# An attention and MoE kernel: where the second matmul's sums of batch 0 lie in PSUM, and one line in the dealing of its pieces

## The chip, the cores and the metric

The kernel runs on one core of a Trainium2 chip. The metric is the device time of one execution in microseconds, as a median over several executions; lower is better. A profile of one execution gives the time of every instruction on each engine: TensorE (PE; its weight loads are shown apart as PEld), VectorE (DVE), ScalarE (ACT), GpSimd (POOL), and the queue of SyncE (SP), which issues most of the transfers.

## The reference, cut to what matters

Attention with a hash mask comes first (4 batches, 8 heads, 768 rows, 64 columns a head). Its output is the input of a two-matmul layer with SiLU between.

```python
def _attn_ref(q, k, v, proj):
    # q, k, v: (4, 8, 768, 64); proj: (64, 6)
    # ... a 6-bit bucket for each row of q and k, by the signs of q@proj and k@proj
    mask = q_bucket[:, :, :, None] == k_bucket[:, :, None, :]
    scores = np.where(mask, scale * np.matmul(q, k.transpose(0, 1, 3, 2)), -1000000000.0)
    # ... softmax
    return np.matmul(attn, v)

def _moe_ref(x, w_in, w_out):          # x: (3072, 512), w_in: (512, 2048), w_out: (2048, 512)
    h = x @ w_in
    g = h * (1.0 / (1.0 + np.exp(-h)))
    return g @ w_out
```

## The kernel before

The kernel is one long software pipeline. The attention is cut into 288 units, nine a head, so 72 units a batch (`BST = 72`). In the loop below, `w` counts them. A unit multiplies one block of exponentials with `v` (`av(w)`) and then makes the scores of the unit three ahead (`score(w + LEAD)`), whose exponential ScalarE takes at once. The layer's work of a batch is cut into pieces and dealt into the units of the next batch: batch 0's pieces go into units 65 to 160 and a few later ones.

PSUM has eight banks, and the kernel splits them by tag: three banks "s" (scores), three banks "m" (first matmuls, projections, transposes) and two banks "o" (attention sums). A bank of a tag is given to the next tile when the tile before it has been read for the last time.

```python
    def score(w):
        # ... pts: one block of 512 columns, or two of 256
        sp = ps.tile([P, 512], F32, tag="s", name="s_ps", bufs=LEAD)      # LEAD = 3
        for jt, c0, n, o0 in pts:
            nc.tensor.matmul(sp[:, o0 : o0 + n], t[:, S + jt * P : S + (jt + 1) * P],
                             t[:, c0 : c0 + n], start=True, stop=True)     # L381
        u = upl.tile([P, 512], F16, tag="u", name="u")
        nc.scalar.activation(out=u, in_=sp, func=AF.Exp, scale=ESC)        # L384
        ut[w] = u
    # ...
    def av(w):
        # ... four matmuls of 65 columns into o_ps, with u of this unit as weights   # L413
```

A piece of the first matmul (`mm1`) holds an "m" bank through four matmuls of 512 columns (or eight of 256), a tanh on ScalarE and a multiplication on VectorE that is issued a unit later:

```python
        def mm1(ci, grp, dts=slice(0, NDT)):
            # ...
                hp = ps.tile([P, 2, f, n // 2], F32, tag="m", name="h_ps", bufs=3)
            # ... matmuls over dt                                                    # L478
            nc.scalar.activation(out=th, in_=hp, func=AF.Tanh, scale=0.5)            # L488
            # ... later: g = (th + 1) * hp on VectorE                                # L491
```

The projection of two later pairs of heads takes two "m" banks at once, one after the other:

```python
    def proj_unit(*pairs):
        # ...
        for c0, w in ((0, 512), (512, S - 512)):
            bp = ps.tile([P, 512], F32, tag="m", name="bp_ps", bufs=3)
            # ... matmuls                                                            # L295
        # ... then one VectorE instruction for each of the two banks                 # L301
```

Batch 0's second matmul treats its larger chunk, 512 of the 768 rows, in four tiles of 128 rows, each a sum over 16 slices of `w_out`, in four pieces of four matmuls. The sum stays in one bank from the first piece to the last, and VectorE then takes it out:

```python
        def whole(t, part):

            if part == 0:
                banks[t] = ps.tile([P, DMODEL], F32, tag="s", name="o2_ps", bufs=3)
            op = banks[t]
            for ft in range(4 * part, 4 * part + 4):
                x = blk[0, ft // NK][:, t // 2, ft % NK, t % 2 * P : (t % 2 + 1) * P]
                nc.tensor.matmul(op, x, w_out16[:, ft, :],                           # L560
                                 start=(ft == 0), stop=(ft == NFT - 1))
            if part == 3:
                o = ops.tile([P, DMODEL], F32, tag="osb", name="osb", bufs=3)
                nc.vector.tensor_scalar(out=o, in0=op, scalar1=half_g, scalar2=None,
                                        op0=ALU.mult)                                # L564
                # ... and a transfer to the output
```

The dealing, with what it does for units 77 to 143 (for batch 0, `moe_list(0)` gives 32 pieces at unit 77):

```python
    for w in range(NW):
        flush()
        for fn in at.pop(w, []):                 # planned work: loads, projections, casts
            fn()
        if w % BST == 1:
            moeq.extend(moe_head())              # six left-over pieces of the batch before
        if w == BST + 5 or w % BST == 11 and w > 2 * BST:
            credit = 0.5
            moeq.extend(moe_list(w // BST - 1))
        keep = 3 if w >= NW - 12 else 0
        left = BST - w % BST
        n = -(-(len(moeq) - keep) // left) if len(moeq) > keep else 0
        in_head = w > 2 * BST and w % BST < 11
        credit += max(len(moeq) - keep, 0) / left
        skip = credit < 0.999 or w % QST in ((20, 21) if w > 2 * BST else (24, 25))
        if w > 2 * BST and w % BST < 11:
            skip = w % BST in (0, 2, 5, 7, 10)
        if n == 1 and len(moeq) - keep < left and skip:
            n = 0
        credit -= n
        for _ in range(n):
            moeq.popleft()()
        av(w)
        if w + LEAD < NW:
            score(w + LEAD)
```

Two more lines matter for what follows. `x_unit(p)` turns the attention's output of head pair `p` into `xT`, the input of the first matmul, by a transposing transfer of the SP queue (L448), for pair 7 planned at unit 146. `mm1` of batch 1 begins at unit 155 and reads `xT` of pairs 4 to 7.

Of the kernel before, what the change touches and what calls it, by code (L numbers as in the profile page):

```python
# [9 lines left out]
F32 = mybir.dt.float32  # L10
# [7 lines left out]
def kernel(  # L18
# [13 lines left out]
    NT, DMODEL = out.shape  # L32
    DFF = moe_w_in.shape[1]
    P = 128
# [23 lines left out]
    ps = ctx.enter_context(tc.tile_pool(name="ps", bufs=1, space=bass.MemoryType.PSUM))  # L58
# [316 lines left out]
    def score(w):  # L375
        h, pts = parts(w)
        p, par = divmod(h, 2)
        t = QKA[p % NSL] if par == 0 else QKB[p % NSL]
        sp = ps.tile([P, 512], F32, tag="s", name="s_ps", bufs=LEAD)
# [6 lines that stand above are left out]
# [68 lines left out]
    def flush():  # L454
        for fn in after:
            fn()
        after.clear()

    def moe_units(b):
# [55 lines left out]
        banks, kept = {}, {}  # L515
# [37 lines left out]
        def whole(t, part):  # L553

            if part == 0:
                banks[t] = ps.tile([P, DMODEL], F32, tag="s", name="o2_ps", bufs=3)
            op = banks[t]
            for ft in range(4 * part, 4 * part + 4):
                x = blk[0, ft // NK][:, t // 2, ft % NK, t % 2 * P : (t % 2 + 1) * P]
# [6 lines that stand above are left out]
                dst = out[b * S : (b + 1) * S, :].rearrange("(p t) n -> p t n", p=P)  # L566
                nc.sync.dma_start(out=dst[:, t, :], in_=o)
# [13 lines left out]
        if b == 0:  # L581
            big = [lambda t=t, part=part: whole(t, part) for t in range(4) for part in range(4)]
        else:
            big = [lambda n=n, t=t: product(0, n, t)
                   for n in (1, 2, 6, 5, 3, 7, 4) for t in range(2)]
            first[13] = then(first[13], (0, 1, lo))
            for grp, c in ((0, (0, 1, hi)), (1, (0, 2, hi)), (3, (0, 4, lo)), (4, (0, 3, lo))):
                second[grp] = then(second[grp], c)
            for i, c in ((2, (0, 2, lo)), (4, (0, 4, hi)), (5, (0, 3, hi))):
                big[i] = then(big[i], c)  # L590
# [17 lines left out]
    def moe_head():  # L608
        units, late[:6] = late[:6], []
        return units  # L610

    def moe_list(b):


        first, second, big, small = moe_units(b) if b else first_units
        if b == 0:
            units = first + spread(second, big[:8])
            late[:] = big[8:] + small
            return units
        units = spread(first[:-3], late) + [big[0]] + first[-3:] + [big[1]]  # L620
        for i, c in enumerate("ababaababababa"):
            units.append((second, big)["ab".index(c)][("ababaababababa"[:i].count(c)) + 2 * (c == "b")])
        late[:] = big[8:] + small
        return units
# [205 lines left out]
    BST = 8 * NU  # L830
# [104 lines left out]
    moeq = deque()  # L935
    credit = 0.0
# [4 lines left out]
    for w in range(NW):  # L941
        flush()
        for fn in at.pop(w, []):
            fn()
        if w % BST == 1:
            moeq.extend(moe_head())
# [4 lines that stand above are left out]
        left = BST - w % BST  # L951
        n = -(-(len(moeq) - keep) // left) if len(moeq) > keep else 0
        in_head = w > 2 * BST and w % BST < 11
        credit += max(len(moeq) - keep, 0) / left
        skip = credit < 0.999 or w % QST in ((20, 21) if w > 2 * BST else (24, 25))
        if w > 2 * BST and w % BST < 11:
            skip = w % BST in (0, 2, 5, 7, 10)
        if n == 1 and len(moeq) - keep < left and skip:
            n = 0
        credit -= n  # L960
        for _ in range(n):
            moeq.popleft()()
        av(w)
        if w + LEAD < NW:
            score(w + LEAD)
# [38 lines left out]
```

## Time and profile before

The median is 295.47 us (295.32 to 295.55 over three executions). The profiled span is 293.8 us.

| engine | busy us | share of the span | instructions |
|---|---|---|---|
| PE | 286.4 | 97% | 2934 |
| PEld | 196.9 | 67% | 2934 |
| DVE | 202.9 | 69% | 402 |
| ACT | 225.0 | 77% | 428 |
| POOL | 204.7 | 70% | 241 |

Busy time of PE is modelled with the matmuls overlapping in its pipeline. So a busy PE is not a PE at its peak, and a wait of some tenths of a microsecond partly disappears under the end of the matmul before it. The distance between the starts of two consecutive instructions shows such a wait whole. In the lists of waits, the engine named last is the one whose signal came last. The lists in order of time give the start in us from the beginning of the span, the busy time in us, engine, line, operation, tiles (out<-in) and the number of instructions merged into the line.

### The profile page before, as it was taken

The page shows a single profiled execution, that of the slowest core. Times are in us where ns is not written, and L with a number is a line of the kernel's source. Part 1 is how long each engine was busy: PE and PEld are TensorE (multiplying, and loading weights), DVE is VectorE, ACT ScalarE, POOL GpSimd, SP SyncE. Part 2 cuts the span into 40 slices and gives each one's busy share as a digit, 9 for nine tenths or more (in the row PEclk, how much of TensorE's full clock was granted, in tenths as well). Part 3 has the DMA queues.
Part 4 walks back from the last instruction along what each step waited for, and adds up shares of the span by engine and source line. Part 5 has one row for each costly group of instructions (what it writes and reads, how often), then busy time and mean ns, then how long its engine had stood idle before and what let it go on. Part 6 is the DMA issues. An engine that isn't in the chain of part 4 may idle for free.

```text
span 293.8 us, 7729 instructions
## 1 busy us (share of the span) xinstructions
PE 286.4 (97%) x2934; PEld 196.9 (67%) x2934; DVE 202.9 (69%) x402; ACT 225.0 (77%) x428; POOL 204.7 (70%) x241
## 2 busy tenths in 40 slices
PE   8999999999998999999999999999999999999995
PEld 3666765555666665567666888656668887666884
DVE  6788868899886464855798447975557749777332
ACT  5999989998987776877887786878888855788400
POOL 8789999379997945999357992579999860264400
PEclk9999999999999999999999999999999999999999
DMA  7999998979979249882199326203120212101114
GB/s 200 242 222 213 220 154 119 228 114 149 208 116 205 69 76 208 165 152 57 41 188 126 62 67 143 100 22 37 36 48 0 65 29 68 49 12 36 39 64 134
DMA packets 105861, 32.91 MB, mean 112 GB/s; under 512 B 90912, under 2 KB 105312, under 8 KB 105824
## 3 DMA queue, kind: packets, MB, share of 16 engines
q1 hardware_dynamic: 101440, 28.23, 48.9%
q0 software_dynamic: 4224, 4.19, 9.2%
q8 instruction: 23, 0.38, 0.6%
q14 instruction: 14, 0.11, 0.1%
q10 hardware_dynamic: 160, 0.00, 0.0%
HBM read 27.27 MB, written 6.29 MB: 114 GB/s over the span
## 4 chain that ended last, share of the span: by engine, by line
PE 89%; DVE 4%; ACT 3%; issue 1%; DMA 1%; SPq 0%; DVEq 0%; ACTq 0%
PE h_ps L478 21%; PE s_ps L381 19%; PE o_ps L530 13%; PE o_ps L413 12%; PE o_ps L793 6%; PE h_ps L687 5%; PE o_ps L560 5%; PE bp_ps L295 3%; ACT u L384 2%; PE tp_ps L199 2%; DMA k_row<-in_k_dram 1%; PE bp_ps L315 1%; ACT th L488 1%; DVE tx L660 1%; DVE osb L542 1%
## 5 line engine op out<-in xcount | busy, mean ns | idle before, releaser
L384 ACT ACTIVATE u<-s_ps 128x512 f16<-128x512 f32 x288 | 157.0, 606 | 28.7 <-PE s_ps L381 28.2
L413 PEld LDWEIGHTS <-u 128*128 128x128 f16 x1152 | 67.3, 98 | 38.1 <-ACT u L384 9.4
L413 PE MATMUL o_ps<-vv,u 128*128 128x65 f16 x1152 | 82.4, 194 | 0.6 <-ACT u L384 0.4
L478 PE MATMUL h_ps<-xT,win 128*128 128x512 f16 (+1 forms) x384 | 75.1, 326 | 0.0
L491 DVE SCALAR_TENSOR_TENSOR g<-th,h_ps 128x512 f16<-128x512 f32 x72 | 48.5, 681 | 37.3 <-ACT th L488 36.9
L381 PE MATMUL s_ps<-qka 128*128 128x512 f16 x192 | 52.6, 326 | 0.8 <-DVE osb L564 0.4
L381 PE MATMUL s_ps<-qkb 128*128 128x512 f16 x192 | 53.0, 326 | 0.2 <-ACT u L384 0.2
L488 ACT ACTIVATE th<-h_ps 128x512 f32<-128x512 f32 x72 | 43.8, 608 | 11.0 <-PE h_ps L478 7.8
L478 PEld LDWEIGHTS <-win 128*128 128x128 f16 x384 | 37.5, 98 | 17.9 <-issue 0.4
L530 PEld LDWEIGHTS <-g 128*128 128x128 f16 x336 | 32.8, 98 | 7.0 <-issue 0.3
L433 POOL TENSOR_TENSOR x_pr<-osum,rec 128x384 f16<-128x384 f32 x23 | 19.7, 858 | 23.9 <-DVE rec L432 22.9
L265 POOL TENSOR_SCALAR qka<-qk 64x1536 f16<-64x1536 f32 x15 | 22.0, 1465 | 15.5 <-DVE qk L260 8.4
L265 POOL TENSOR_SCALAR qkb<-qk 64x1536 f16<-64x1536 f32 x15 | 22.1, 1471 | 1.2
L530 PE MATMUL o_ps<-wt,g 128*128 128x256 f16 x168 | 21.8, 272 | 0.1
L530 PE MATMUL o_ps<-wout,g 128*128 128x256 f16 x168 | 21.4, 272 | 0.0
L276 POOL TENSOR_TENSOR vsa<-v_sb 128x192 f32<-128x192 f32 x32 | 18.9, 592 | 0.0
L274 POOL CAST vv<-v_sb 128x384 f16<-128x384 f32 x32 | 16.7, 522 | 0.5
L560 PE MATMUL o_ps<-wout,g 128*128 128x512 f16 x64 | 16.4, 379 | 0.6 <-ACT u L384 0.5
L717 POOL TENSOR_TENSOR gs<-qka,gs 128x768 f16<-128x768 f16 x2 | 3.3, 1646 | 18.4 <-ACT qka L704 15.7
L260 DVE STREAM_TRANSPOSE qk<-k_blk 128x768 f32<-128x768 f32 x10 | 16.0, 1597 | 0.0
L381 PEld LDWEIGHTS <-qka 128*128 128x128 f16 x192 | 15.4, 97 | 0.8 <-ACT qka L252 0.6
L260 DVE STREAM_TRANSPOSE qk<-q_blk 128x768 f32<-128x768 f32 x10 | 15.9, 1586 | 0.0
(123 smaller groups left out, 441.7 us busy)
## 6 DMA issues: line engine op xcount, KB each, us to landing
v_sb<-in_v_dram SPq DMA_DIRECT2D x15, 384.0 KB
out_dram<-osb SPq DMA_DIRECT2D x16, 256.0 KB
q_blk<-in_q_dram SPq DMA_DIRECT2D x40, 96.0 KB
k_blk<-in_k_dram SPq DMA_DIRECT2D x40, 96.0 KB
win<-in_moe_w_in_dram POOLq DMA_DIRECT2D x4, 512.0 KB, 8.0
wout<-in_moe_w_out_dram POOLq DMA_DIRECT2D x4, 512.0 KB, 6.9
q_sb<-in_q_dram SPq DMA_DIRECT2D x5, 384.0 KB
k_sb<-in_k_dram SPq DMA_DIRECT2D x5, 384.0 KB
```

What stands on the lines that cost most here:

```text
L260: nc.vector.transpose(out=dst, in_=qk_sb[p, "qk"[n]])
L265: nc.gpsimd.tensor_scalar(out=dst[rows, :], in0=qk32[p][rows, :], scalar1=CS, scalar2=1.0, op0=ALU.mult, op1=ALU.mult)
L276: nc.gpsimd.tensor_tensor(out=sa, in0=src[:, 0:3], in1=src[:, 3:6], op=ALU.add)
L381: nc.tensor.matmul(sp[:, o0 : o0 + n], t[:, S + jt * P : S + (jt + 1) * P], t[:, c0 : c0 + n], start=True, stop=True)
L384: nc.scalar.activation(out=u, in_=sp, func=AF.Exp, scale=ESC)
L413: nc.tensor.matmul(o_ps[h][:, c0 // P + i, :], u[:, o0 + i * P : o0 + (i + 1) * P], vv[:, jt, :], start=(not direct(h) and w % NU == 0 and ...
L433: (nc.vector if direct(h) else nc.gpsimd).tensor_tensor(out=x_pr[p][:, :, par * D : (par + 1) * D], in0=o[:, 0:NJ, 0:D], in1=rec[:, :, Non ...
L478: nc.tensor.matmul(hp[:, :, j, :], w_in16[:, dt, ft * P : (ft + 1) * P], xT[4 * b + dt][:, c0 : c0 + n] .rearrange("d (r c) -> d r c", r=2 ...
L488: nc.scalar.activation(out=th, in_=hp, func=AF.Tanh, scale=0.5)
L491: nc.vector.scalar_tensor_tensor(out=g, in0=th.rearrange("p r f c -> p r (f c)"), scalar=1.0, in1=hp.rearrange("p r f c -> p r (f c)"), op ...
L530: nc.tensor.matmul(op[:, t, :], x[:, k, t * P : (t + 1) * P], y[:, k], start=(first and k == 0), stop=True, skip_group_check=True)
L560: nc.tensor.matmul(op, x, w_out16[:, ft, :], start=(ft == 0), stop=(ft == NFT - 1))
```

## The change

The diff changes the tag of `whole`'s sums from "s" to "m", so that the scores of the units in which such a sum is open keep all three of their banks, and the sum shares the three "m" banks with the first matmuls. It also changes the dealing in batch 1: the credit of units 79 to 143 is reckoned as if one more piece were in the list, and unit 78 is told to deal one piece. This is meant to have one piece dealt beforehand.

```diff
         def whole(t, part):
 
             if part == 0:
-                banks[t] = ps.tile([P, DMODEL], F32, tag="s", name="o2_ps", bufs=3)
+                banks[t] = ps.tile([P, DMODEL], F32, tag="m", name="o2_ps", bufs=3)
             op = banks[t]
@@
         left = BST - w % BST
         n = -(-(len(moeq) - keep) // left) if len(moeq) > keep else 0
         in_head = w > 2 * BST and w % BST < 11
-        credit += max(len(moeq) - keep, 0) / left
+        ahead = BST + 6 < w < 2 * BST
+        credit += max(len(moeq) + ahead - keep, 0) / left
         skip = credit < 0.999 or w % QST in ((20, 21) if w > 2 * BST else (24, 25))
         if w > 2 * BST and w % BST < 11:
             skip = w % BST in (0, 2, 5, 7, 10)
         if n == 1 and len(moeq) - keep < left and skip:
             n = 0
         credit -= n
+        if w == BST + 6:
+            n = 1
         for _ in range(n):
             moeq.popleft()()
         av(w)
```

## The prediction

> **What bounds the kernel now.** I read the page first. PE is busy for 97% of the span, and the chain of work that ended last is 89% PE, so time that PE loses anywhere is time of the kernel, and nothing else is worth much.
>
> ```profile
> PE 286.4 (97%) x2934; PEld 196.9 (67%) x2934; DVE 202.9 (69%) x402; ACT 225.0 (77%) x428; POOL 204.7 (70%) x241
> ...
> PE 89%; DVE 4%; ACT 3%; issue 1%; DMA 1%; SPq 0%; DVEq 0%; ACTq 0%
> ```
>
> Second, the line of the changed matmuls (L560): they run from 80 to 122 us, so only that stretch, and what follows from it, can move. Third, PE's waits in 80 to 122 us. There are three:
>
> ```profile
> PE o_ps L560 <- ACT u L384: 0.5, 1, 0.5
> PE s_ps L381 <- DVE osb L564: 0.4, 1, 0.4
> PE s_ps L381 <- ACT u L384: 0.3, 1, 0.3
> ```
>
> All are waits for an "s" bank: two end when an exponential has read a score bank, one when L564 has emptied a sum. As busy time runs over the pipeline's end, the true loss is read in the list in order of time, as the distance between starts:
>
> ```profile
> 87.99 0.28 PE L413 MATMUL o_ps<-vv,u 128*128 128x65 f16 x4
> 88.56 0.38 PE L381 MATMUL s_ps<-qka 128*128 128x512 f16 x1 [0.29 <-ACT u L384]
> ...
> 93.20 0.38 PE L381 MATMUL s_ps<-qka 128*128 128x512 f16 x1
> 94.08 1.02 PE L560 MATMUL o_ps<-wout,g 128*128 128x512 f16 x4 [0.50 <-ACT u L384]
> ...
> 106.49 0.29 PE L413 MATMUL o_ps<-vv,u 128*128 128x65 f16 x4
> 107.17 0.38 PE L381 MATMUL s_ps<-qka 128*128 128x512 f16 x1 [0.40 <-DVE osb L564]
> ...
> 108.59 0.28 PE L413 MATMUL o_ps<-vv,u 128*128 128x65 f16 x4
> 108.71 0.38 PE L381 MATMUL s_ps<-qka 128*128 128x512 f16 x1
> 108.93 1.03 PE L560 MATMUL o_ps<-wout,g 128*128 128x512 f16 x4
> ...
> 113.03 0.38 PE L381 MATMUL s_ps<-qkb 128*128 128x256 f16 x2
> 113.51 1.02 PE L560 MATMUL o_ps<-wout,g 128*128 128x512 f16 x4
> ```
>
> The triple at 108.59 is undisturbed: 0.12 us from L413 to the next score, 0.22 from a score to the next instruction. Against that the four places lose 0.57 - 0.12 = 0.45, 0.88 - 0.22 = 0.66, 0.68 - 0.12 = 0.56 and 0.48 - 0.22 = 0.26 us. **Sum: 1.93 us.** The last is too short for the list of waits; that it also waits for a bank is my reading (L564 empties the sum before it at 112.77, for 0.69 us).
>
> **What the Trainium skill says.** (1) "Perfetto Trace Analysis", Optimization Strategy: the same gap repeating on the engine that should be saturated "can mean there isn't enough SBUF/PSUM for the next tile to be allocated". The four gaps agree. (2) The same page, Matmuls: independent groups should rotate through banks so that the emptying of one overlaps the next group. Here a sum that stays open for 13 units (units 113 to 126 for the first) takes one of three banks out of that rotation. (3) "TensorE: Matmul & The Clock Gate", Back-to-back issue gap, gives 512/2.4 + 2.5, about 216 ns, for an isolated gap of 512 columns, and 131 ns sustained; the trace shows 0.22 us from a score to the next instruction, so the first. (4) "Perfetto Trace Analysis", What "DMA-bound" means: an issuing sequencer can be the bound when its track is solid with transfers. The SP queue here is nearly solid from 84 to 122 us; I use this below.
>
> **The change, part by part.**
>
> *Part 1, the tag.* It removes no instruction and adds none. With all three "s" banks for the scores, the four waits above have no cause. At 88.56 two score banks are in use and the third would be free. At 94.08 the sum would take an "m" bank: the first sum left its own with L564 at 92.11 to 92.76, and only one first matmul (91.87) is under way. At 107.17 and 113.51 no first matmul is under way at all. Gain: 1.93 us.
>
> *What it adds in "m".* One bank is now a sum's, two remain. A first matmul holds one from its start until L491 ends: in the time-ordered list, 81.77 to 84.16 and 88.77 to 91.16, so 2.4 us. Such pieces come every fourth unit, 3.1 us apart (81.77, 84.86), so two banks suffice. The tight place is the projection of unit 132 (95.74 us), which wants two banks. It begins two units after a first matmul in the new order (part 2). From that first matmul's start: 0.86 + 0.12 + 0.22 to the end of its unit, 0.34 for the next, so the projection begins at 1.54; its second bank is wanted 0.9 us later (half-way of the 1.43 us from 95.74 to 97.17, weighted by columns), at about 2.44, and the bank is free at about 2.4. Cost: 0 to 0.2, I take 0.1 us.
>
> *Part 2, the dealing.* I worked the loop by hand. At unit 77 the credit is 0.5 + 32/67 = 0.978, below 0.999: no piece. At unit 78 it is 0.978 + 32/66 = 1.46: the kernel before **already deals a piece at 78**, so the line that forces n = 1 changes nothing. The larger credit does: up to unit 100 both deal alike; from there each piece comes earlier, at 102, 104, ... 122 for 103, 105, ... 124, then two to four units earlier. In particular the sixth small-chunk piece moves from 134 to 130, ahead of the projection of 132, and the last piece of the batch from 142 to 140. PE's sum is the same. So units 141 to 144 now have no piece, four in a row where there were two. A unit without a piece is 0.12 + 0.22 = 0.34 us of PE, but an exponential takes 0.54 us in a row (two in 1.08). Counting from the start of the score for unit 143, its exponential starts 0.41 later (91.72 after the score at 91.31) and lasts 0.60: done at 1.01, the next at 1.55. PE wants them at 0.90 and, after a first wait of 0.16 with 0.05 for the signal, at 1.40. Waits: 0.16 + 0.20. Cost: **0.36 us**. Unit 145 has a piece again.
>
> *What runs beside it.* ACT is busy for 31.56 of the 42 us from 80 to 122, DVE for 26.23: no new bound. The SP queue is different. After the projection's bits (98.2 us) it issues eight transfers of bits, eight of q and k blocks and two transposes without a pause; the transpose that makes `xT` of pair 7 is issued at 112.81 and its last signals come at 115.62. The first matmul of unit 155 starts at 116.25 and wants that part with its fourth instruction, at 116.90. **Slack: 1.28 us.** PE will come there 1.93 - 0.36 - 0.1, about 1.5 us earlier. The queue moves only with the projection: gains before it 0.45 + 0.66, but one more piece (0.86) now lies ahead of it and the 0.1 for the bank, so 0.15 earlier. Expected wait: 1.5 - 1.28 - 0.15, so 0 to 0.1; I take 0.1 us.
>
> Sum: -1.93 + 0.36 + 0.1 + 0.1 = -1.37 us. I give back 0.1 for small waits that a shifted order makes and I can't place: 295.47 - 1.27 = **294.2 us**.
>
> **The rivals.** (A) *The wait moves to "m"*: projection or first matmuls wait for L491 or L564 instead. For it: the second bank above misses by hundredths of a microsecond, and VectorE's 1.6 us transposes (L260) can delay L491: the one wanted at 93.54 started at 94.09. Against it: 3.1 us between such pieces against 2.4 of use. It would return 0.5 to 1.5 us: 294.6 to 295.6. (B) *The SP queue sets unit 155*: if its transfers don't move at all or lengthen (single issues range from 0.59 to 1.8 us), all gain above 1.28 is lost, or more: 294.2 to 295.2. (C) *The units 141 to 144 cost more*, up to four times 0.2 us, if ScalarE enters them behind: 294.6. (D) *Nothing of 1.93 comes back*: 293.6, if C and the others vanish.
>
> **Range and chances.** The repeats spread over 0.23 us, so size decides. D gives the low end, 293.5. A and B together would nearly cancel the gain; 295.1 covers most of that. A 2% change is 5.9 us, three times all the loss in the stretch: faster 0.01, same 0.98, slower 0.01.
>
> **What would show it.** Right: the three waits for "s" banks are gone from PE's list; L560 never starts later than 0.25 us after a score; a wait for ACT of some 0.2 us at L413 just ahead of unit 145; unit 155's first matmul starts at about 115 us instead of 116.25; the rest is shifted alike. Wrong: PE waiting for DVE at L295 or L478 by over 0.3 us (A), PE waiting for the transfer of `xT` (B), or the shift at 116.25 absent at the end, which would say that a later bound has taken it.

## The result, and the profile after

The changed kernel takes 294.62 us (median; 294.08 to 294.95) against 295.51 us for the kernel before in the same comparison. The ratio of the mean times is 0.9964, with a 95% interval of 0.9949 to 0.9979: faster by 0.4%, and the median lies within the predicted range of 293.5 to 295.1 us.

The page of the changed kernel, with its engines and its chain:

```profile
PE 286.5 (98%) x2934; PEld 196.6 (67%) x2934; DVE 203.3 (69%) x402; ACT 224.8 (77%) x428; POOL 204.6 (70%) x241
...
PE 90%; DVE 5%; ACT 3%; issue 1%; POOL 0%; DVEq 0%; ACTq 0%; POOLq 0%
```

Nothing changed in kind: each engine has as many instructions as before, its busy time is the same to 0.4 us, and PE is still the bound. The span fell from 293.8 to 292.7 us. PE's list of waits over the whole changed kernel shows why:

```profile
PE warm_ps L125 <- POOL warm L114: 1.0, 1, 1.0
PE o_ps L413 <- ACT u L384: 0.4, 1, 0.4
PE h_ps L687 <- DVE part L701: 0.3, 1, 0.3
PE s_ps L381 <- ACT u L384: 0.2, 1, 0.2
PE s_ps L381 <- DVE qka L252: 0.2, 1, 0.2
```

The three waits for a score bank that the prediction showed are gone; the wait of L381 for ACT that is left lies far behind the changed stretch, at 233.19 us, and the kernel before has it too, at 234.23. That is not yet the whole account, because this list misses what hides under a matmul's pipeline. The list in order of time for PE of the changed kernel shows new losses at three places, and in its last line the first matmul of unit 155, which began at 116.25 before:

```profile
71.97 0.29 PE L413 MATMUL o_ps<-vv,u 128*128 128x65 f16 x4
72.10 0.38 PE L381 MATMUL s_ps<-qkb 128*128 128x512 f16 x1
72.60 1.02 PE L478 MATMUL h_ps<-xT,win 128*128 128x512 f16 x4
...
105.31 0.38 PE L381 MATMUL s_ps<-qka 128*128 128x256 f16 x2
105.77 0.29 PE L413 MATMUL o_ps<-vv,u 128*128 128x65 f16 x4
105.90 0.38 PE L381 MATMUL s_ps<-qka 128*128 128x512 f16 x1
106.26 0.29 PE L413 MATMUL o_ps<-vv,u 128*128 128x65 f16 x4
...
115.21 1.03 PE L478 MATMUL h_ps<-xT,win 128*128 128x512 f16 x4
```

A score is normally followed 0.22 us later by the next instruction. At 72.60 it is 0.50 us, so 0.28 to 0.29 are lost (the expectations below round this to 0.30); at 105.77 it is 0.46, so 0.24; at 106.26 it is 0.36, so 0.14 to 0.15. The first of these is at unit 102, the other two at the L413 of units 143 and 144. What these two wait for is seen at their weight loads, from 104 to 107 us of the changed kernel:

```profile
PEld L413 <- ACT u L384: 0.6, 2, 0.3
```

**How the runs are compared below.** The first unit of a profiled execution starts between 0.19 us earlier and 0.36 us later than in the kernel before, and that offset stays for the rest of the span. It is as large as some of the effects. So each stretch is measured inside its own trace: the start of a unit's first L413 less that of unit 60's, compared with the same difference in the kernel before. "By unit 160" then is all that batch 0's pieces did. From there to unit 287, and likewise ahead of unit 60, no run moves by more than 0.03 us, so a gain there reaches the end, and differences of a tenth can be told apart. Each of these figures comes from one profiled execution.

| kernel | by unit 160, us | median us | ratio, 95% interval |
|---|---|---|---|
| the change | -1.24 | 294.62 | 0.9964 (0.9949 to 0.9979) |
| new bank alone | -1.92 | 294.16 | 0.9948 (0.9928 to 0.9969) |
| new dealing alone | -0.11 | 295.47 | 0.9993 (0.9984 to 1.0001) |
| tiles 0 and 1 alone in the new bank | -1.43 | 293.95 (one execution) | |
| new bank, larger credit in 104 to 131 | -1.55 | 294.02 | 0.9934 (0.9913 to 0.9955) |
| the change, its additional piece at 79 | -1.97 | 293.72 | 0.9923 (0.9901 to 0.9944) |
| new bank, additional piece at 79, none at 99 | -2.36 | 293.00 | 0.9924 (0.9910 to 0.9937) |

Each ratio is that of the mean times, against the kernel before on the same chip, whose median was 295.51, 295.80 or 295.39 us. The intervals of the change and of the new bank alone overlap, so their difference rests on the traces; so does that between the last two rows.

### The profile page after: what moved, and what is told of

Its sections match the earlier page's. It is cut to its first block, busy times and chain, and to the rows that moved or that the text cites. A ratio compares the mean times of both kernels' runs of the same rounds, so it can differ in the third digit from the quotient of the medians.

```text
span 292.7 us, 7759 instructions
## 1 busy us (share of the span) xinstructions
PE 286.5 (98%) x2934; PEld 196.6 (67%) x2934; DVE 203.3 (69%) x402; ACT 224.8 (77%) x428; POOL 204.6 (70%) x241
## 4 chain that ended last, share of the span: by engine, by line
PE 90%; DVE 5%; ACT 3%; issue 1%; POOL 0%; DVEq 0%; ACTq 0%; POOLq 0%
PE h_ps L478 21%; PE s_ps L381 19%; PE o_ps L530 13%; PE o_ps L413 12%; PE o_ps L793 6%; PE h_ps L687 5%; PE o_ps L560 5%; PE bp_ps L295 3%; ACT u L384 2%; PE tp_ps L199 2%; PE warm_ps L125 1%; PE bp_ps L315 1%; DVE tx L660 1%; DVE osb L542 1%; PE bp_ps L239 1%
## 5 line engine op out<-in xcount | busy, mean ns | idle before, releaser
L413 PEld LDWEIGHTS <-u 128*128 128x128 f16 x1152 | 67.2, 98 | 39.0 <-ACT u L384 10.1
L413 PE MATMUL o_ps<-vv,u 128*128 128x65 f16 x1152 | 82.4, 194 | 0.7 <-ACT u L384 0.4
L478 PE MATMUL h_ps<-xT,win 128*128 128x512 f16 (+1 forms) x384 | 75.1, 326 | 0.1
L491 DVE SCALAR_TENSOR_TENSOR g<-th,h_ps 128x512 f16<-128x512 f32 x72 | 48.5, 680 | 37.0 <-ACT th L488 36.5
L381 PE MATMUL s_ps<-qkb 128*128 128x512 f16 x192 | 53.2, 326 | 0.2 <-ACT u L384 0.2
L381 PE MATMUL s_ps<-qka 128*128 128x512 f16 x192 | 52.5, 326 | 0.2 <-DVE qka L252 0.2
L478 PEld LDWEIGHTS <-win 128*128 128x128 f16 x384 | 37.5, 98 | 18.1 <-issue 0.4
L381 PEld LDWEIGHTS <-qka 128*128 128x128 f16 x192 | 15.4, 97 | 0.8 <-ACT qka L252 0.6
```

Source lines behind the costliest of these rows:

```text
L413: nc.tensor.matmul(o_ps[h][:, c0 // P + i, :], u[:, o0 + i * P : o0 + (i + 1) * P], vv[:, jt, :], start=(not direct(h) and w % NU == 0 and ...
L478: nc.tensor.matmul(hp[:, :, j, :], w_in16[:, dt, ft * P : (ft + 1) * P], xT[4 * b + dt][:, c0 : c0 + n] .rearrange("d (r c) -> d r c", r=2 ...
L491: nc.vector.scalar_tensor_tensor(out=g, in0=th.rearrange("p r f c -> p r (f c)"), scalar=1.0, in1=hp.rearrange("p r f c -> p r (f c)"), op ...
```

## The experiments

**The new bank alone.** The kernel before with one word changed:

```diff
-                banks[t] = ps.tile([P, DMODEL], F32, tag="s", name="o2_ps", bufs=3)
+                banks[t] = ps.tile([P, DMODEL], F32, tag="m", name="o2_ps", bufs=3)
```

> The new bank alone, with the dealing of the kernel before. Theory (banks): the four waits for a score bank, 0.45 + 0.66 + 0.56 + 0.26 = 1.93 us, all go, and the two waits that the new dealing made in the changed kernel, 0.30 us ahead of the first matmul of unit 102 and 0.39 us in units 143 and 144, do not come: 1.9 us faster than the kernel before (about 293.6), so 0.7 us faster than the changed kernel. Rival (the dealing is needed, since otherwise the first matmul of unit 134 follows the projection of unit 132 with a sum and two projection banks open and waits for VectorE): a new wait of 0.3 to 1.0 us at unit 134, about 294.3 to 295.

Measured: -1.92 us by unit 160. It comes in four steps, at units 124 (0.45), 130 (0.65), 145 (0.56) and 152 (0.27), just where the four gaps were. At the largest of them, ahead of the second sum's first piece, PE now goes on after 0.22 us where it was 0.88:

```profile
92.93 0.38 PE L381 MATMUL s_ps<-qka 128*128 128x512 f16 x1
93.15 1.03 PE L560 MATMUL o_ps<-wout,g 128*128 128x512 f16 x4
```

There is no loss at unit 134, against the rival. The four gaps were waits for a score bank, and the new bank alone takes all of them away. What the change has less than this, 0.68 us, is what its dealing costs. The ten executions with the new bank alone spread widely, from 293.42 to 295.51 us, and two of them were no faster than the kernel before; no run shows why.

**The new dealing alone.** The changed kernel with the sums back in the score banks (tag "s" again).

> The new dealing alone, with the sums in score banks as before. Theory (banks): the wait of 0.45 us goes, as the two units without a piece (122, 123) go; those of 0.66 and 0.26 us stay; the end of the batch waits for VectorE or ScalarE for 0.5 us as before or some 0.2 more; and the 0.30 us at unit 102 comes: within 0.4 us of the kernel before (295.1 to 295.9). Rival (the dealing brings most of the gain): 0.6 us or more faster than before.

Measured: -0.11 us by unit 160, and a ratio whose interval holds 1. PE's waits from 78 to 125 us in this run:

```profile
PE o_ps L560 <- ACT u L384: 0.5, 1, 0.5
PE s_ps L381 <- ACT u L384: 0.2, 1, 0.2
```

The first is the wait of 0.66 us at the second sum's first piece, as before: it belongs to the bank, whatever the dealing. The second is at unit 142, where a score starts 0.51 us after L413 in place of 0.12, so 0.39 are lost. The 0.29 us at unit 102 are there too, though the sums lie in score banks, so the dealing makes them. The rival falls: the dealing brings nothing of weight.

**The forced piece.** The kernel before has a piece in unit 78 as well, a matmul of L478 at 52.59 us, and the changed kernel has the same one at 52.80. So the hand-worked loop was right: n is 1 already when the line sets it to 1, and the line does nothing. The larger credit reads as if it were made to go with a piece that really is additional. That can be had one unit later:

```diff
-        ahead = BST + 6 < w < 2 * BST
+        ahead = BST + 7 < w < 2 * BST
@@
-        if w == BST + 6:
+        if w == BST + 7:
             n = 1
```

> The changed kernel with the forced piece and the larger credit one unit later, so that a piece really is dealt in addition, at unit 79, and all later units that have a piece are those of the kernel before, except 142. Theory: the wait of 0.49 us for ScalarE at unit 81, which both kernels have, goes, the 0.30 us at unit 102 goes, the 0.39 us at the end stay: 1.93 + 0.49 - 0.39, about 2.0 us faster than the kernel before (293.5). Rival: ScalarE is behind in units 76 to 82, and the tanh of a first matmul that comes two units earlier puts it further behind, so the wait at 81 only moves to the next units: 1.5 us faster than before (294.0).

Measured: -1.97 us by unit 160. PE's order of time in the run with the new bank alone shows what there was to gain, ahead of the L413 at 54.92 us (the kernel before has the same wait, at 54.75):

```profile
54.14 0.38 PE L381 MATMUL s_ps<-qkb 128*128 128x512 f16 x1
54.92 0.29 PE L413 MATMUL o_ps<-vv,u 128*128 128x65 f16 x4 [0.40 <-ACT u L384]
```

That is 0.78 us where 0.22 is normal, 0.56 lost. Another 0.13 are lost ahead of the L413 of unit 79. With the additional piece both gaps are closed, and 0.26 us are lost two units after the larger one instead (57.06 us). By unit 90 the extra piece, four matmuls or 0.86 us of PE, has cost only 0.41 us, so 0.45 were won. Theory and rival are both half right here: some of the wait went, some moved. The loss at unit 102 is gone, as unit 103 has its piece again; the loss in units 143 and 144 is there, 0.24 and 0.15, as unit 142 again has none.

**The larger credit in the middle alone.** The new bank, and against the changed kernel

```diff
-        ahead = BST + 6 < w < 2 * BST
+        ahead = BST + 31 < w < BST + 60
@@
-        if w == BST + 6:
-            n = 1
```

> The new bank, with the larger credit in units 104 to 131 alone: unit 103 keeps its piece, the small chunk's sixth first matmul comes at unit 131, just ahead of the projection of 132, and the last piece stays at unit 142. Theory: no wait at 102 and none at 143 and 144, but the projection's second bank is now wanted 2.1 us after the start of a first matmul that holds it for 2.4 us: a wait for VectorE of 0.2 to 0.4 us at the projection, 1.5 to 1.7 us faster than before (about 293.9). Rival (the m banks have room to spare there): no wait, 1.9 us faster.

Measured: -1.55 us. Against the bank alone it loses 0.28 us between units 131 and 132 and 0.09 at unit 155. PE of this run, in order of time:

```profile
94.21 1.04 PE L478 MATMUL h_ps<-xT,win 128*128 128x256 f16 x8
...
95.20 0.38 PE L381 MATMUL s_ps<-qka 128*128 128x512 f16 x1
95.51 1.78 PE L295 MATMUL bp_ps<-qk,pw 128*32 128x512 f32 x16
...
114.61 1.12 PE L478 MATMUL h_ps<-xT,win 128*128 128x512 f16 x4
```

The waits of PE's weight loads from 90 to 120 us name the first:

```profile
PEld bp_ps L295 <- DVE g L491: 1.0, 1, 1.0
```

The projection takes 1.78 us in place of 1.50: with a first matmul in the unit just ahead, its second bank is still held until L491 has read it. This is rival A of the prediction, and it is real, but only one unit nearer than the change goes. The second loss is rival B. The four matmuls of unit 155 take 1.12 us in place of 1.03: the fourth started at 115.35, and the transfer of pair 7's `xT` had landed at 115.31. In the change it landed at 115.48 and was wanted at 115.86. Here chance has a part: one issue of the projection's bits (L346, 103.00 us) took 1.04 us in this run and 0.72 in the change, and it delays all that the queue issues after it. This is more than the 0.09 us lost.

**Tiles 0 and 1 alone.** The dealing of the kernel before, and

```diff
-                banks[t] = ps.tile([P, DMODEL], F32, tag="s", name="o2_ps", bufs=3)
+                banks[t] = ps.tile([P, DMODEL], F32, tag="m" if t < 2 else "s", name="o2_ps", bufs=3)
```

> The dealing of the kernel before; the sums of tiles 0 and 1 in the new bank, those of tiles 2 and 3, which are made at the head of the next batch, in score banks as before. Theory: the waits of 0.45, 0.66 and 0.56 us go, that of 0.26 us ahead of the first piece of tile 3 stays: 1.67 us faster than before in the trace from unit 80 to unit 160, against 1.92 us with all four. Rival (the gap of 0.26 us, which the list of waits does not name, is not a wait for a bank): 1.92 us.

Measured: -1.43 us. PE in order of time:

```profile
105.32 0.38 PE L381 MATMUL s_ps<-qka 128*128 128x512 f16 x1
105.77 1.02 PE L560 MATMUL o_ps<-wout,g 128*128 128x512 f16 x4
...
111.41 0.38 PE L381 MATMUL s_ps<-qkb 128*128 128x256 f16 x2
111.90 1.02 PE L560 MATMUL o_ps<-wout,g 128*128 128x512 f16 x4
```

The gap ahead of tile 3 stays (0.49 us against 0.22, so 0.27), and with the new bank alone it goes. So it is a wait for a bank, though no list of waits names it. The theory missed 0.24 us: at 105.77 the first piece of tile 2 now starts 0.45 us after a score, 0.23 too late. With its sum in the new bank it does not, so it waits for a score bank itself.

**The best order found.** The additional piece at 79, and in exchange none at 99, again against the changed kernel:

```diff
-        ahead = BST + 6 < w < 2 * BST
+        ahead = BST + 7 < w < BST + 28
@@
-        if w == BST + 6:
+        if w == BST + 7:
             n = 1
+        if w == BST + 27:
+            n = 0
```

> The new bank, a piece really dealt in addition at unit 79, and in exchange none at unit 99; from unit 103 on the dealing is that of the kernel before, so unit 142 keeps its piece. Theory: the four waits for a score bank go (1.93 us), of the wait for ScalarE at unit 81 some 0.45 us go, as in the run with the additional piece at 79, the three first matmuls in a row of units 98 to 100 are spread, and no wait comes at 102, at the projection or at 143 and 144: 1.93 + 0.45, about 2.4 us faster than the kernel before, 0.45 us faster than the new bank alone. The transfer that sets the first matmul of unit 155 moves with the projection and should land 0.4 us before it is wanted. Rival: with PE 2.4 us earlier at unit 155 the transfer queue, which issues without a pause, no longer follows, and all above 1.9 us is lost in a wait for it.

Measured: -2.36 us by unit 160, and 293.00 us. PE has no wait from 78 to 122 us that the list names. The transfer landed at 114.05 and was wanted at 114.35: the queue followed, with 0.30 us in hand where 0.4 was expected.

This beats both the kernel before and the changed one: the interval of its ratio does not overlap that of the change. By the ratios it cannot be told from the run with the additional piece at 79 and the changed dealing (0.9924 and 0.9923); that it is 0.39 us better rests on the trace.

## Why the prediction was right, point by point

The total was right: 1.27 us forecast, 1.24 by the trace and 0.89 by the medians (the ratio's interval stands for 0.6 to 1.5 us). The mechanism was the one named. The terms did less well: a loss that was not foreseen is about as large as three costs that did not come, so the agreement within 0.03 us is luck.

- **Four waits for a score bank, 1.93 us.** Right: -1.92 with the bank alone, in the four steps foretold. The reading that the unnamed fourth gap is a wait for a bank held too.
- **The line at unit 78 does nothing.** Right. The larger credit alone changes the order, from unit 102 on.
- **Units 143 and 144, 0.36 us.** Right: 0.24 + 0.15 = 0.39 (0.16 + 0.20 foretold), and the same again with the additional piece at 79, where the last piece is at unit 140 too. The waits stand at the L413 of units 143 and 144, not just ahead of unit 145.
- **The projection's second bank, 0.1 us.** Did not come: 0.32 us from the score to the projection, against 0.31 before, and 1.50 us for its matmuls in both. The mechanism was right: the weight loads of L295 waited 0.6 us for L491, which cost PE nothing here; one unit nearer they wait 1.0 us, and it costs 0.28.
- **The transfer queue, 0.1 us.** Did not come: 0.38 us were in hand, in part by luck. PE came 1.24 us earlier, not 1.5. The projection began 0.06 us later than before, not 0.15 earlier, as the loss at unit 102 lies ahead of it. The transfer landed 0.34 us earlier all the same, because four issues took less time (the first line is the kernel before, the second the changed one):

```profile
104.78 3.17 SPq L92 DMA_DIRECT2D q_blk<-in_q_dram  x4
105.03 2.71 SPq L92 DMA_DIRECT2D q_blk<-in_q_dram  x4
```

  One of the four took 1.10 us in the kernel before and 0.64 in the changed one; no run shows why. With 3.17 us again the transfer would have come 0.08 us too late, by an estimate from these numbers. So the slack of 1.28 us, read in one execution, was smaller by 0.46 than it is when no issue is slow. That PE waits when the transfer is late is right, as the 0.09 us in another order show.
- **The failing step: "Such pieces come every fourth unit, 3.1 us apart (81.77, 84.86), so two banks suffice."** That looked only at the stretch with an open sum. The new order also puts a first matmul at unit 102, after those of units 98, 99 and 100, and there all three "m" banks were busy, with no sum among them. VectorE of the changed kernel:

```profile
70.35 0.60 DVE L356 TENSOR_SCALAR qkb<-bits,sc 13x768 f16<-13x768 f16 x1
70.88 0.20 DVE L426 COPY vsum<-o_ps 128x65 f32<-128x65 f32 x1
...
71.90 1.25 DVE L491 SCALAR_TENSOR_TENSOR g<-th,h_ps 128x512 f16<-128x512 f32 x2
```

  The tanh of the first of those pieces, which began at 68.37, was done at 70.03, but VectorE had the projection's bits and a head's sums in its queue and came to it at 71.90. The bank was free only at about 72.55, so PE lost 0.29 us. Before, the piece came at unit 103 and found it free. So -1.92 + 0.29 + 0.39 = -1.24, and not -1.93 + 0.36 + 0.1 + 0.1 = -1.37. The 0.1 that was held back for waits not placed brings the forecast to -1.27; the wait at unit 102 alone is three times as large.

## What to carry to other kernels

A sum that stays open over many steps takes a bank out of whatever ring it is put in: put it where the ring has room, and reckon the room from each bank's time in use, up to the end of the last reader, the reader's own queue included, and at the densest place of the order, not at the usual one. When a change joins a new buffer with a new order, run each alone: here the buffer brought 1.92 us and the order took back 0.68. A condition in a schedule that "adds one" is to be worked through by hand, since this one added nothing where it was put, and at unit 79, with none at unit 99, a piece that really was additional was worth 0.45 us more.

## What the runs showed that was not expected

The list of waits understates a wait of PE by the pipelined end of the matmul before: 0.5, 0.4 and 0.3 us were 0.66, 0.56 and 0.45 by the distance of starts, and 0.26 and 0.29 us were not named at all. And the start of the first unit alone differs by 0.55 us between profiled executions (9.10 to 9.65 us), more than most effects here, so they show only within a trace.
